# Maxima's rows on ScalarE and GpSimd, a split accumulator copy, additions moved in the tail, and weight slices prepared every five half steps

## The chip, the core and the metric

The kernel runs on one core of a Trainium2 chip. The metric is device time in microseconds of one execution. The core's engines work side by side, each through its own list of instructions in a fixed order: TensorE (PE; its weight loads are shown as PEld), VectorE (DVE), ScalarE (ACT), GpSimd (POOL), and SyncE (SP), which here issues the DMA transfers. An instruction starts when everything ahead of it on its engine has started and the semaphores that it waits for have arrived.

## What is computed

A transformer block with conditioning, for one sequence of 2048 tokens of width 512 in fp32, with 32 heads of 16 and an MLP of width 1792:

```python
mod = (_silu(c) @ w_mod).reshape(c.shape[0], 6, 1, -1)
sa, ca, ga, sb, cb, gb = (mod[:, i] for i in range(6))
h = _layernorm(x) * (1 + ca) + sa
x = x + ga * (softmax((q @ k.T) * 16 ** -0.5) @ v) @ wo      # q, k, v = h @ wqkv, by head
h = _layernorm(x) * (1 + cb) + sb
x = x + gb * (mish(h @ w1 + b1) @ w2)                         # mish(u) = u * tanh(softplus(u))
```

## The kernel before

The products of QKV and MLP are made of fp32 values split in a high and a low part (`hi_copy` and `lo_sub`, lines 93 to 98), three matmuls each.

Attention runs in 512 steps: 32 groups (`n`), one for each of 4 query blocks of 512 and each of 8 groups of 4 heads, with 16 key chunks of 128 each. In step `t` TensorE makes four score products of chunk `t` (L512), four products for the maxima of a later group (L471), which run 20 steps ahead (`PRO`), and the value products of step `t - 2` (L540). Beside the products on half of the array it runs halves of six matmuls of QKV or MLP work (L132). A step is counted in the profile from one bunch of L540 to the next.

The maxima of a group (VectorE, L473) are gathered (`neg_max`), transposed on TensorE (L490) and turned into two rows, high and low part of the negated maximum (`max_rows`: mh L494, mt L495). Four small DMAs (L501) put them into the rows of `qa` that belong to the queries, so that the score product subtracts the maximum by itself: `j` is the pair of heads, `s` the half of the array. The first score of the group uses `j = 0, s = 1`.

When the 16 chunks of a group are added up in a PSUM bank (`acc`), `evac` copies it to `ot` (L554, ScalarE), and DMAs bring sums and rows from `ot` to where the division is made, one or two steps later.

Work that is not TensorE's is hung on half steps, `h = 2t` or `2t + 1` (`at(h, f)`); the order in which hooks run is the order of the instructions on every engine. The weights of the output projection and the MLP are split once, in slices of 128x512 (`prep_unit`): load (L653), three operations on POOL five half steps later (gate L657, L95, L98), and the store to memory (L660) nine half steps after the load. The 32 slices are started by `start_preps`, `PREP = 4` half steps apart, or later where a buffer is not free. The blocks of the MLP (`first_loads`, one for each query block) load them again (L666). `load_pair` brings the keys and queries of a pair of heads (L294, L303).

After the last step `tail` finishes query block 3 alone: attention output, layer norm, MLP. There TensorE also runs ten products that were held back from block 2 (`held`), two at a time into a PSUM pair, each added to `y` by VectorE (L889); `put_h` splits the layer norm's output between them (L712 on ACT, L95 on POOL, L98 on DVE).

Of the kernel before, what the change touches and what calls it, by code (L numbers as in the profile page):

```python
# [18 lines left out]
def adaln_block(ctx: ExitStack, tc: tile.TileContext, x, wqkv, wo, w1, b1, w2, c, w_mod, out):  # L19
    nc = tc.nc  # L20
    P = 128
# [18 lines left out]
    CUT1, CUT2 = (0, 1), (2, 3)  # L40
    LOV = ((1,), (), (1, 3), (1, 3))
    PREP = 4
    CREDIT = 7.5
    HCAP = 10.0

# [439 lines left out]
    def max_rows(n, mm):  # L485
        t = ring(2)
        cols = mm.rearrange("p a v q -> p (a v q)")
        for g in range(2):
            r = slice(64 * g, 64 * g + 64)
            nc.tensor.transpose(t[:32, g, :64], cols[r], ident[r, r])  # L490
        pt = t[:32, :, :64]
        mh, mt = [ap.tile([32, P], F32R, tag=n_, name=n_, bufs=1) for n_ in ("mh", "mt")]
        halves = [m.rearrange("p (g q) -> p g q", g=2) for m in (mh, mt)]
        nc.vector.tensor_scalar_mul(halves[0], pt, -1.0)  # L494
        nc.vector.scalar_tensor_tensor(halves[1], halves[0].bitcast(F32), lows[:32], pt, op0=ALU.mult, op1=ALU.subtract)  # L495

        def put():
            for j in range(2):
                for s in range(2):
                    o = (2 * s + j) * 8  # L500
                    nc.sync.dma_start(  # L501
                        qa[(2 * n + j) % NR][64 * s + 48:64 * s + 50, :].rearrange("v (s q) -> v s q", s=4).bitcast(F32),
                        mt[o:o + 8, :].bitcast(F32))
        at(2 * (16 * n + 16 - PRO) + 3, put)
# [43 lines left out]
    def evac(n):  # L548
        qb, g = divmod(n, G)
        t1 = 16 * (n + 1) + 1  # L550
        if g == 0:
            o_hl[qb] = [ap.tile([P, DK, TB], F32R, tag=f"o_{i}", name="o_hl", bufs=1) for i in range(2)]
        ot = ap.tile([P, TB], F32, tag="ot", name="ot", bufs=1)
        nc.scalar.copy(ot, accs.pop(n))  # L554
# [24 lines left out]
        if g % 2 == 1 or n == NIT - 2:  # L579
            r = slice(0, P if g % 2 else 64)  # L580

            oh, ol = o_hl[qb]
            k, d, e = (2 * t1 + 42, 7, 11) if g == 1 else (2 * t1 + 11, 0, 0) if hurry else (2 * t1 + 23, 4, 8)
            at(k, lambda: nc.gpsimd.tensor_mul(od[r], od[r], rb[r]))
            at(k + d, lambda: hi_copy("p", oh[r, g // 2, :], od[r]))
            at(k + e, lambda: lo_sub("p", ol[r, g // 2, :], od[r], oh[r, g // 2, :]))
# [59 lines left out]
                nc.vector.tensor_copy(modc[:, v - 1, 2 * o:2 * o + 2], acc[:, :2])  # L646
        return fin

    def prep_unit(h, third, scr, src, gate):

        hl = (qp if third else pw).tile([P, 2, D], F32R, tag="vq" if third else "hl", name="hl", bufs=1 if third else 2)
        raw = hl[:, 1, :].bitcast(F32)
        nc.sync.dma_start(raw.rearrange("p (k m) -> p k m", m=src.shape[-1]) if len(src.shape) == 3 else raw, src)  # L653

        def split():
            if gate is not None:
                nc.gpsimd.tensor_mul(raw, raw, gates[gate])  # L657
            hi_copy("p", hl[:, 0, :], raw)
            lo_sub("p", hl[:, 1, :], raw, hl[:, 0, :])
            at(clear(h + 9), lambda: nc.sync.dma_start(scr.rearrange("p v m -> p (v m)"),  # L660
                                                        hl.rearrange("p v m -> p (v m)").bitcast(F32)))
        at(h + 5, split)
# [131 lines left out]
    def block(qb, t0):  # L794
# [8 lines left out]
        def first_loads(h):  # L803
            load(h + 1, wos, load_wo, range(DK))
            load(h + 2, y, lambda i: load_y(qb, i), range(4))
            load(h + 9, w1s, load_w1, range(2))
            load(h + 10, w2s, load_w2, range(NW - DK))
            done["w"] = h + 3

        def wo_unit(i, tag):  # L810
# [179 lines left out]
    def tail():  # L990
# [48 lines left out]
        for k in range(DK):  # L1039
            for i in range(4):  # L1040
                nc.tensor.transpose(accs[k][:, i * P:(i + 1) * P], xn[i][:, k * P:(k + 1) * P], ident)
        for k in range(DK):
            put_h(hh, hl, accs[k], k, True)
        fins += held((6, 7))
        for f in fins:
            f(None)
        for f in held((8, 9)):
            f(None)
        for f in range(6):
            w2s[f] = load_w2(f)  # L1050
        po = [ring(2) for _ in range(2)]
# [3 lines left out]
        for u in range(FT + LAG):  # L1055
# [12 lines left out]
            if f >= 0:  # L1068
                a_h, a_l = act.pop(f)
                w = w2s.pop(f)  # L1070
                for i in range(4):
                    s = slice(i * P, (i + 1) * P)
                    for j, (l, r) in enumerate(((a_h, 0), (a_h, 1), (a_l, 0))):
                        nc.tensor.matmul(po[i // 2][:, i % 2, :], l[:, s], w[:, r, :], start=(f == 0 and j == 0),  # L1074
                                         stop=(f == FT - 1 and j == 2))
                    if f == FT - 1 and i % 2:
                        for q in (i - 1, i):
                            nc.vector.tensor_add(y[q], po[q // 2][:, q % 2, :], y[q])
                            r = 4 * last + q
                            nc.sync.dma_start(out[r * P:(r + 1) * P, :], y[q])  # L1080
                if f + 6 < FT:
                    w2s[f + 6] = load_w2(f + 6)

# [289 lines left out]
```

## Time and profile before

| what | value |
| --- | --- |
| three timed runs | 1693.45, 1697.57, 1698.18 us (median 1697.57) |
| the profiled execution | 1693.26 us, span 1691.5 us |
| granted TensorE clock, mean | 0.996 |
| TensorE busy | 1660.6 us, 98% of the span |
| VectorE, ScalarE, GpSimd busy | 1429.9, 1327.1, 898.0 us |

The span runs from the first to the last instruction; the device time has 1.8 us around it. A row of a timeline gives the start in us, the duration in us, the engine, the line, the operation, what is written and read, the shape and the number of instructions that the row joins; in brackets stands how long the engine was idle ahead of it and what ended that. A row of waits gives the total in us, how many times, and the longest. SPq rows are DMA issues on SP's queue.

### The profile page before, as it was taken

To read this page: it belongs to the slowest core of one execution; us is meant where nothing else is said; L and a number is where in the kernel's file an instruction comes from. 1 tells how busy PE (TensorE), PEld (TensorE's weight loads), DVE (VectorE), ACT (ScalarE), POOL (GpSimd) and SP (SyncE) were. 2 spreads that over 40 slices of the span, in tenths; PEclk is the share of its full clock that TensorE was granted. 3 is DMA by queue.
4 is the path that set the end of the run, shared out by engine and by line. 5 is a ranking of instruction groups with operands and counts; after the bars stand their busy time and mean duration, and the time that the engine had idled before them with its cause. 6 is when DMAs were issued, how large, how long until landed. Compare 5 with 4: busy or idle time off the path is not lost.

```text
span 1691.5 us, 32962 instructions
## 1 busy us (share of the span) xinstructions
PE 1660.6 (98%) x12316; PEld 921.7 (54%) x12316; DVE 1429.9 (85%) x2362; ACT 1327.1 (78%) x2559; POOL 898.0 (53%) x906
## 2 busy tenths in 40 slices
PE   6999999999999999999999999999999999999998
PEld 5755665554435455555555555555555555554687
DVE  6898898887998888988888888889888888881577
ACT  6247777777778898888889898888888898889264
POOL 5155215565504388755525498654535597646432
PEclk9999999999999999999999999999999999999999
DMA  7767457777772342434353644334442535332362
GB/s 249 192 224 215 120 159 213 250 226 226 232 210 63 111 123 74 127 80 149 86 133 74 197 105 99 99 109 123 117 103 79 176 95 131 93 107 82 132 218 74
DMA packets 113992, 240.03 MB, mean 142 GB/s; under 512 B 24048, under 2 KB 49648, under 8 KB 107784
## 3 DMA queue, kind: packets, MB, share of 16 engines
q1 hardware_dynamic: 113832, 237.92, 49.6%
q8 instruction: 97, 1.59, 0.4%
q14 instruction: 63, 0.52, 0.1%
HBM read 179.95 MB, written 51.44 MB: 137 GB/s over the span
## 4 chain that ended last, share of the span: by engine, by line
PE 92%; DVE 3%; DMA 2%; ACT 2%; SPq 1%; issue 1%; POOL 0%; DVEq 0%; ACTq 0%; POOLq 0%
PE bk L540 30%; PE ring L471 23%; PE ring L512 22%; PE bk L132 9%; PE bk L126 3%; PE ring L126 3%; PE ring L1074 2%; DVE mx L473 1%; ACT pr L520 1%; DMA xt<-in_A_x 1%; SPq L318 0%; DMA qa<-mt 0%; PE bk L1006 0%; DMA vg<-vscr 0%; PE ring L842 0%
## 5 line engine op out<-in xcount | busy, mean ns | idle before, releaser
L473 DVE TENSOR_REDUCE mx<-ring 128x1 f32<-128x512 f32 x2048 | 1276.1, 684 | 161.5 <-PE bk L132 104.9
L520 ACT ACTIVATE pr<-ring 128x512 f32<-128x512 f32 x2048 | 1090.2, 605 | 232.0 <-PE bk L132 168.8
L471 PE MATMUL ring<-ka,qa 64*128 64x512 f32 x2048 | 778.7, 427 | 0.5
L512 PE MATMUL ring<-qa,ka 64*128 64x512 f32 x2048 | 723.0, 397 | 7.8 <-ACT pr L520 4.6
L471 PEld LDWEIGHTS ring<-ka,qa 64*128 64x128 f32 x2048 | 366.5, 184 | 407.9 <-DVE mx L473 356.2
L540 PE MATMUL bk<-pr,vg 128*32 128x512 f32 x4096 | 545.9, 605 | 0.0
L512 PEld LDWEIGHTS ring<-qa,ka 64*128 64x128 f32 x2048 | 374.1, 184 | 120.8 <-ACT pr L520 35.6
L132 PE MATMUL bk<-h,w 64*128 64x512 f32 x1008 | 280.7, 410 | 0.0
L132 PE MATMUL bk<-w,a_h 64*128 64x512 f32 x576 | 194.8, 417 | 0.6 <-ACT pr L520 0.4
L132 PEld LDWEIGHTS bk<-h,w 64*128 64x128 f32 x1008 | 171.5, 184 | 5.7 <-ACT pr L520 0.4
L540 PEld LDWEIGHTS bk<-pr,vg 128*32 128x32 f32 x4096 | 81.0, 108 | 125.1 <-issue 117.0
L740 POOL TENSOR_SCALAR ee<-hb 128x512 f32<-128x512 f32 x42 | 62.5, 1488 | 96.7 <-ACT hb L734 88.2
L132 PE MATMUL bk<-w,a_l 64*128 64x512 f32 x288 | 113.7, 395 | 0.0
L770 POOL TENSOR_TENSOR ee<-ee,rr 128x512 f32<-128x512 f32 x42 | 53.9, 1284 | 111.6 <-ACT rr L761 111.4
L132 PEld LDWEIGHTS bk<-w,a_h 64*128 64x128 f32 x576 | 95.3, 185 | 5.2 <-ACT pr L520 1.5
L132 PE MATMUL bk<-w,o_hl 64*128 64x512 f32 x288 | 79.7, 409 | 0.0
L98 POOL TENSOR_TENSOR a_l<-hb,a_h 128x512 fp32r<-128x512 f32 x53 | 71.7, 1354 | 4.4
L893 POOL TENSOR_TENSOR y<-yd,y 128x512 f32<-128x512 f32 x40 | 51.4, 1285 | 35.5 <-ACT yd L892 35.3
L754 POOL TENSOR_SCALAR rr<-ee 128x512 f32<-128x512 f32 x42 | 26.1, 622 | 60.0 <-ACT ee L746 59.9
L132 PE MATMUL bk<-h_h,wl 64*128 64x512 f32 x168 | 57.5, 423 | 0.0
L95 POOL TENSOR_SCALAR a_h<-hb 128x512 fp32r<-128x512 f32 x53 | 36.3, 684 | 39.9 <-DVE hb L768 38.3
L774 POOL TENSOR_TENSOR hb<-hb,rr 128x512 f32<-128x512 f32 x42 | 54.5, 1298 | 3.3
(205 smaller groups left out, 1840.9 us busy)
## 6 DMA issues: line engine op xcount, KB each, us to landing
ka<-kscr SPq DMA_DIRECT2D x124, 384.0 KB
w<-w2scr SPq DMA_DIRECT2D x56, 512.0 KB
w<-w1scr SPq DMA_DIRECT2D x46, 512.0 KB
vg<-vscr SPq DMA_DIRECT2D x32, 552.0 KB
qa<-qscr SPq DMA_DIRECT2D x124, 100.0 KB
kscr<-qh SPq DMA_DIRECT2D x16, 512.0 KB
qscr<-qh SPq DMA_DIRECT2D x32, 256.0 KB
hl<-in_B_w SPq DMA_DIRECT2D x28, 256.0 KB
```

Of the source, the lines that this page charges most:

```text
L98: (nc.gpsimd if eng == "p" else nc.vector).tensor_sub(lo, src, hi.bitcast(F32))
L126: nc.tensor.matmul(acc, l, r, start=start, stop=stop)
L132: i = nc.tensor.matmul(acc, l[64 * g:64 * g + 64], r[64 * g:64 * g + 64], start=start, stop=stop)
L471: nc.tensor.matmul(pm, qt[64 * s:64 * s + 64, qs * P:(qs + 1) * P], kt[64 * s:64 * s + 64, kb * TB:(kb + 1) * TB], start=True, stop=True)
L473: return nc.vector.tensor_reduce(out=mxs[n][:, s, 4 * j + qs, kb:kb + 1], in_=pm, op=ALU.max, axis=AX.X)
L512: nc.tensor.matmul(p_, kt[64 * s:64 * s + 64, kc * P:(kc + 1) * P], qt[64 * s:64 * s + 64, :], start=True, stop=True)
L520: e = nc.scalar.activation(pr, p_, AF.Exp, scale=SCALE)
L540: nc.tensor.matmul(accs[n][32 * h:32 * h + 32, :], vgs[n][:, o:o + 32], pts.pop((t, h)), start=(kc == 0), stop=(kc == 15))
L740: nc.gpsimd.tensor_scalar_min(buf("ee", 2), b["hb"], HCAP)
L770: nc.gpsimd.tensor_mul(ee, ee, rr)
L774: nc.gpsimd.tensor_mul(hb, hb, rr)
L893: nc.gpsimd.tensor_add(y[i], yd, y[i])
```

## The change

It has these parts.

- `max_rows`: the negated rows are copied by ScalarE from PSUM, and mh and mt are then made by POOL (two operations of 32x128) in place of two operations on VectorE. Of the four DMAs those for `s = 1` are issued first.
- `evac`: the first 256 columns of the accumulator are copied by VectorE, the others by ScalarE.
- `tail`: the additions of the held products 4 and 5 stand before `put_h` and those of 6 and 7 behind it, and each output row tile is added when its own products are done.
- `start_preps`: `EARLY = 28` slices, five half steps apart (the first six as before); the last four are prepared when the MLP's memory is open, from half step 256 on, in tiles of their own.
- The keys of group 8's first pair are loaded 8 half steps sooner, and block 0's slices of w1 and w2 20 half steps later.

```diff
     def max_rows(n, mm):
 ...
-        halves = [m.rearrange("p (g q) -> p g q", g=2) for m in (mh, mt)]
-        nc.vector.tensor_scalar_mul(halves[0], pt, -1.0)
-        nc.vector.scalar_tensor_tensor(halves[1], halves[0].bitcast(F32), lows[:32], pt, op0=ALU.mult, op1=ALU.subtract)
+        mc = mt.bitcast(F32)
+        nc.scalar.activation(mc.rearrange("p (g q) -> p g q", g=2), t[:32, :, :64], AF.Copy, scale=-1.0)
+        nc.gpsimd.tensor_scalar_mul(mh, mc, lows[:32])
+        nc.gpsimd.tensor_add(mt, mc, mh.bitcast(F32))

         def put():
-            for j in range(2):
-                for s in range(2):
+            for s in (1, 0):
+                for j in range(2):
...
-        nc.scalar.copy(ot, accs.pop(n))
+        acc = accs.pop(n)
+        nc.vector.tensor_copy(ot[:, :TB // 2], acc[:, :TB // 2])
+        nc.scalar.copy(ot[:, TB // 2:], acc[:, TB // 2:])
...
-    def prep_unit(h, third, scr, src, gate):
+    def prep_unit(h, third, scr, src, gate, hl=None):
-        hl = (qp if third else pw).tile(...)
+        hl = hl if hl is not None else (qp if third else pw).tile(...)
...
         def first_loads(h):
-            load(h + 9, w1s, load_w1, range(2))
-            load(h + 10, w2s, load_w2, range(NW - DK))
+            late = 20 if qb == 0 else 0
+            load(h + 9 + late, w1s, load_w1, range(2))
+            load(h + 10 + late, w2s, load_w2, range(NW - DK))
...
     def tail():
+        for f in fins:
+            f(None)
         for k in range(DK):
             put_h(hh, hl, accs[k], k, True)
-        fins += held((6, 7))
-        for f in fins:
-            f(None)
-        for f in held((8, 9)):
-            f(None)
+        for js in ((6, 7), (8, 9)):
+            for f in held(js):
+                f(None)
...
-                    if f == FT - 1 and i % 2:
-                        for q in (i - 1, i):
-                            nc.vector.tensor_add(y[q], po[q // 2][:, q % 2, :], y[q])
+                    if f == FT - 1:
+                        nc.vector.tensor_add(y[i], po[i // 2][:, i % 2, :], y[i])
...
-        if i == len(preps):
+        if i == EARLY:
-        then = clear(max(h + PREP, puts[0] + 1 if len(puts) > 2 - (not three) else 0))
+        then = clear(max(h + (PREP if not three else 5), puts[0] + 1 if len(puts) > 2 - (not three) else 0))
...
     def prep_step(t):
+            room = [mst["p"].tile([P, 2, 2, D], F32R, tag=f"h2_{v}", name="late", bufs=1) for v in range(2)]
+            for i, args in enumerate(preps[EARLY:]):
+                h = 2 * t + 12 + 3 * i
+                at(h, lambda h=h, i=i, args=args: prep_unit(h, False, *args, room[i // 2][:, i % 2]))
...
-            at(32 * (n - 2) + (15 if n % 2 == 0 else 9), lambda n=n: load_pair(2 * n))
+            at(32 * (n - 2) + (7 if n == 8 else 15 if n % 2 == 0 else 9), lambda n=n: load_pair(2 * n))
```

The order of the instructions shows where these stand. First SP around the maxima's rows of group 6. `hl` is a weight slice (loaded from `in_B_w`, stored to `w2scr`), `qa<-mt` are the rows, `qscr` and `kscr` hold queries and keys. Before:

```order
L660 DMA w2scr<-hl 128x1024
L458 DMA vg<-vscr 128x1104
L252 DMA qscr<-ql 8x16x512
L252 DMA qscr<-qh 8x16x512 x2
L653 DMA hl<-in_B_w 128x512
L660 DMA w2scr<-hl 128x1024
L501 DMA qa_108<-mt 2x4x128 x2
L501 DMA qa_109<-mt 2x4x128 x2
```

After:

```order
L459 DMA vg<-vscr 128x1104
L253 DMA qscr<-ql 8x16x512
L253 DMA qscr<-qh 8x16x512 x2
L663 DMA w2scr<-hl 128x1024
L656 DMA hl<-in_B_w 128x512
L502 DMA qa_108<-mt 2x4x128
L502 DMA qa_109<-mt 2x4x128
L502 DMA qa_108<-mt 2x4x128
L502 DMA qa_109<-mt 2x4x128
```

Between two groups' rows SP issues fewer slices, a load stands directly ahead of the rows where a store stood, and the rows of the two pairs alternate.

POOL in a block, around the same rows of group 11. `hb`, `rr` and `ee` are the pieces of mish, `a_h` and `a_l` the parts of its result. Before:

```order
L773 TENSOR_TENSOR hb<-hb,ee 128x512
L774 TENSOR_TENSOR hb<-hb,rr 128x512
L740 TENSOR_SCALAR ee<-hb 128x512
L95 TENSOR_SCALAR a_h<-hb 128x512
L98 TENSOR_TENSOR a_l<-hb,a_h 128x512
```

After:

```order
L776 TENSOR_TENSOR hb<-hb,ee 128x512
L777 TENSOR_TENSOR hb<-hb,rr 128x512
L495 TENSOR_SCALAR mh<-mt,lows 32x128
L496 TENSOR_TENSOR mt<-mt,mh 32x128
L743 TENSOR_SCALAR ee<-hb 128x512
L96 TENSOR_SCALAR a_h<-hb 128x512
L99 TENSOR_TENSOR a_l<-hb,a_h 128x512
```

The two new operations stand in the middle of the mish of two tiles.

ScalarE at the copy of group 10's accumulator (`bk` is the bank), with the semaphores that each instruction waits for: DMAHW is a DMA queue, the others are engines. Before:

```order
L520 ACTIVATE pr_0_1182<-ring 128x512 [waits PE_49]
L554 COPY ot<-bk 128x512 [waits DMAHW4_49,DMAHW5_49,DMAHW3_49,DMAHW6_49,DMAHW2_49,PE_49]
L520 ACTIVATE pr_2_1151<-ring 128x512 [waits PE_49]
L758 ACTIVATE rr<-ee,two 128x512 [waits Pool_49]
L520 ACTIVATE pr_2_1159<-ring 128x512 [waits PE_49]
```

After:

```order
L521 ACTIVATE pr_0_1183<-ring 128x512 [waits PE_49]
L557 COPY ot<-bk 128x256 [waits DMAHW4_49,DMAHW5_49,DMAHW3_49,DMAHW6_49,DMAHW2_49,DVE_49]
L521 ACTIVATE pr_2_1152<-ring 128x512 [waits PE_49]
L761 ACTIVATE rr<-ee,two 128x512 [waits Pool_49]
L521 ACTIVATE pr_2_1160<-ring 128x512 [waits PE_49]
```

The half copy keeps the place of the whole one. It waits for VectorE (its half, L556) where the whole copy waited for TensorE.

Last, VectorE in the tail: `y` additions of held products and the four subtractions of `put_h`. Before:

```order
L889 TENSOR_TENSOR y_5265<-ring,y_5265 128x512
L889 TENSOR_TENSOR y_5266<-ring,y_5266 128x512
L98 TENSOR_TENSOR h_17735<-hf_17766,h_17734 128x512
L98 TENSOR_TENSOR h_17735<-hf_17770,h_17734 128x512
L98 TENSOR_TENSOR h_17735<-hf_17774,h_17734 128x512
L98 TENSOR_TENSOR h_17735<-hf_17778,h_17734 128x512
L889 TENSOR_TENSOR y_5267<-ring,y_5267 128x512
L889 TENSOR_TENSOR y_5268<-ring,y_5268 128x512
```

After:

```order
L893 TENSOR_TENSOR y_5280<-ring,y_5280 128x512
L893 TENSOR_TENSOR y_5281<-ring,y_5281 128x512
L99 TENSOR_TENSOR h_17797<-hf_17830,h_17796 128x512
L99 TENSOR_TENSOR h_17797<-hf_17834,h_17796 128x512
L99 TENSOR_TENSOR h_17797<-hf_17838,h_17796 128x512
L99 TENSOR_TENSOR h_17797<-hf_17842,h_17796 128x512
L893 TENSOR_TENSOR y_5278<-ring,y_5278 128x512
L893 TENSOR_TENSOR y_5279<-ring,y_5279 128x512
```

The additions to `y_5267` and `y_5268` (after: `y_5280`, `y_5281`) moved from behind the subtractions to ahead of them. TensorE's list of matmuls is the same before and after.

More of the change, by code (lines that the diff above doesn't have):

```diff
@@ L42, in adaln_block @@
     PREP = 4
+    EARLY = 28
     CREDIT = 7.5
@@ L490, in max_rows @@
             nc.tensor.transpose(t[:32, g, :64], cols[r], ident[r, r])
-        pt = t[:32, :, :64]
         mh, mt = [ap.tile([32, P], F32R, tag=n_, name=n_, bufs=1) for n_ in ("mh", "mt")]
-        halves = [m.rearrange("p (g q) -> p g q", g=2) for m in (mh, mt)]
-        nc.vector.tensor_scalar_mul(halves[0], pt, -1.0)
-        nc.vector.scalar_tensor_tensor(halves[1], halves[0].bitcast(F32), lows[:32], pt, op0=ALU.mult, op1=ALU.subtract)
+        mc = mt.bitcast(F32)
+        nc.scalar.activation(mc.rearrange("p (g q) -> p g q", g=2), t[:32, :, :64], AF.Copy, scale=-1.0)
+        nc.gpsimd.tensor_scalar_mul(mh, mc, lows[:32])
+        nc.gpsimd.tensor_add(mt, mc, mh.bitcast(F32))
         def put():
-            for j in range(2):
-                for s in range(2):
+            for s in (1, 0):
+                for j in range(2):
                     o = (2 * s + j) * 8
@@ L647, in mod_unit @@
         return fin
-    def prep_unit(h, third, scr, src, gate):
-        hl = (qp if third else pw).tile([P, 2, D], F32R, tag="vq" if third else "hl", name="hl", bufs=1 if third else 2)
+    def prep_unit(h, third, scr, src, gate, hl=None):
+        hl = hl if hl is not None else (qp if third else pw).tile([P, 2, D], F32R, tag="vq" if third else "hl", name="hl", bufs=1 if third else 2)
         raw = hl[:, 1, :].bitcast(F32)
@@ L1075, in tail @@
                                          stop=(f == FT - 1 and j == 2))
-                    if f == FT - 1 and i % 2:
-                        for q in (i - 1, i):
-                            nc.vector.tensor_add(y[q], po[q // 2][:, q % 2, :], y[q])
-                            r = 4 * last + q
-                            nc.sync.dma_start(out[r * P:(r + 1) * P, :], y[q])
+                    if f == FT - 1:
+                        nc.vector.tensor_add(y[i], po[i // 2][:, i % 2, :], y[i])
+                        r = 4 * last + i
+                        nc.sync.dma_start(out[r * P:(r + 1) * P, :], y[i])
                 if f + 6 < FT:
```

## Prediction

> **What bounds the kernel now.** I read the list of what TensorE waited for first, then the timeline at those places, then the windows, then steps of the attention loop that differ by one instruction only. The page gives the engines' shares, the second view TensorE's waits:
>
> ```profile
> PE 1660.6 (98%) x12316; PEld 921.7 (54%) x12316; DVE 1429.9 (85%) x2362; ACT 1327.1 (78%) x2559; POOL 898.0 (53%) x906
> PE ring L512 <- DMA qa<-mt: 2.5, 1, 2.5
> PE ring L126 <- DVE y L889: 2.4, 1, 2.4
> ```
>
> TensorE is busy 98% of the span and gets the same matmuls in the same order after the change, so only holes in its row can be won or lost. Two are long. The first, at group n=6 (DVE and POOL rows, then SP, then PE):
>
> ```profile
> 377.31 0.34 DVE L495 SCALAR_TENSOR_TENSOR mt<-mh,lows,ring 32x128 fp32r<-32x128 f32 x1 [0.28 <-DVE mh L494]
> 380.57 1.30 POOL L98 TENSOR_TENSOR ql<-ql,qh 128x512 fp32r<-128x512 f32 x1
> 380.71 0.67 SPq L660 DMA_DIRECT2D w2scr<-hl  x1
> 381.51 4.63 SPq L501 DMA_DIRECT2D qa<-mt  x4
> 384.39 0.64 PE L540 MATMUL bk<-pr,vg 128*32 128x512 f32 x4
> 388.43 0.50 PE L512 MATMUL ring<-qa,ka 64*128 64x512 f32 x1 [2.50 <-DMA qa<-mt]
> 390.67 1.93 PE L540 MATMUL bk<-pr,vg 128*32 128x512 f32 x8
> 394.42 1.07 PE L540 MATMUL bk<-pr,vg 128*32 128x512 f32 x8
> ```
>
> The rows of maxima (mt) were ready at 377.65, but SP issued their four DMAs only from 381.51, behind the store of a weight slice, and the score matmul waited 2.50. A step runs from one group of L540 to the next: these two took 6.28 and 3.75, where an ordinary one takes 2.84 (669.11 to 671.95 below). They lose 10.03 − 5.68 = 4.35 us, more than the wait. The second hole is in the tail:
>
> ```profile
> 1599.11 0.69 DVE L98 TENSOR_TENSOR h<-hf,h 128x512 fp32r<-128x512 f32 x1 [3.96 <-POOL h L95]
> 1603.34 2.48 DVE L889 TENSOR_TENSOR y<-ring,y 128x512 f32<-128x512 f32 x4
> 1604.08 0.98 PE L126 MATMUL ring<-w,a_h 128*128 128x512 f32 x2 [2.42 <-DVE y L889]
> 1608.54 2.94 PE L126 MATMUL bk<-h,ka 128*128 128x512 f32 x12
> 388.40:392.40 4.00, 3.97 (x20) 1.55 (x20) 1.98 (x3) 2.17 (x4) 3.83 (x5) 0.61 1.03 193
> 600.90:657.30 56.40, 56.40 (x442) 29.87 (x434) 50.51 (x87) 51.07 (x100) 53.92 (x50) 1.00 0.37 99
> 1604.00:1608.70 4.70, 4.62 (x13) 3.66 (x14) 2.51 (x5) 0.00 (x0) 0.00 (x0) 0.64 0.38 139
> ```
>
> The last three rows are windows; after the busy times of PE, PEld, DVE, ACT and POOL stand the granted TensorE clock, the DMA share and GB/s. Behind both holes the clock is 0.61 and 0.64, against 1.00 in an undisturbed stretch: the slow matmuls there belong to the price of the wait. The Trainium skill (TensorE: Matmul & The Clock Gate, Part 1) puts the fall after an idle window of about 3.4 us. By that, waits of 2.50 and 2.42 would leave the clock alone, and removing them would bring 4.9 us of the 8.35 that the two holes cost. The rows here disagree with it, and I go by them.
>
> **The change part by part.** *SP and the weight slices.* Slices every five half steps, with a buffer reused two half steps later, take the blocked store away from ahead of the maxima's rows; row s=1, which the first score needs, now goes first. This can bring 0 to 4.35. But mt now comes from POOL. In the order of POOL it stands behind the ql row above, which ended at 381.87; with 0.9 for the two new instructions it would be ready at 382.8, with SP free, where the four DMAs began at 381.51 and the second of them released TensorE at 388.4. Only because the prepared slices lie farther apart will POOL be earlier there. I take 3.7: most of it, as the fall of the clock goes with even a partly shortened wait.
>
> *Tail.* The two y additions that free the PSUM pair for the waiting matmuls move ahead of the four subtractions, into the 3.96 us in which VectorE idled until 1599.11. So the 12 matmuls start where TensorE went idle, 1604.08 − 2.42 = 1601.66, and run at full clock: what took 4.46 at 0.64 takes 2.85 (the 12 behind, at 1608.54, take 2.94 with the end of the last). The next 12 start at 1604.51 in place of 1608.54: 4.0 (0 to 4.0). Their h is ready when the subtractions end, before 1604.1. The additions at the very end, one row tile at a time, cover nothing that TensorE waits for: 0.
>
> *Maxima's rows.* An ordinary step, and one with the transposes of the maxima:
>
> ```profile
> 654.72 1.06 PE L540 MATMUL bk<-pr,vg 128*32 128x512 f32 x8
> 655.71 0.23 PE L490 MATMUL ring<-ident,mm 64*32 64x64 f32 x2
> 656.01 0.28 DVE L494 TENSOR_SCALAR mh<-ring 32x128 fp32r<-32x128 f32 x1
> 656.33 0.34 DVE L495 SCALAR_TENSOR_TENSOR mt<-mh,lows,ring 32x128 fp32r<-32x128 f32 x1
> 656.66 1.09 ACT L520 ACTIVATE pr<-ring 128x512 f32<-128x512 f32 x2 [0.33 <-PE ring L512]
> 657.75 0.64 PE L540 MATMUL bk<-pr,vg 128*32 128x512 f32 x4
> 669.11 1.06 PE L540 MATMUL bk<-pr,vg 128*32 128x512 f32 x8
> 671.95 1.06 PE L540 MATMUL bk<-pr,vg 128*32 128x512 f32 x8
> ```
>
> 3.03 against 2.84: 0.19, in which VectorE gave up 0.62. The transposes stay; I leave them half their 0.23, so 0.075 a step and 2.4 over 32 groups is won (0 to 6.1). ScalarE's new copy of 32x128, estimated at 0.25 from 0.374 for 128x256 below, fits its idle 0.33; without that cover it would cost like the copy in the next part, 0.2 a group.
>
> POOL gets two instructions of at most 0.452 each (the row of L850 below is four times as many partitions), 0.9 a group. POOL is 53% busy in all, but 53.92 of 56.40 in the window above, and this returns in three of the four blocks. POOL's first new instruction also waits for ScalarE's copy, with slices, products and mish pieces queued behind it; where POOL comes late, as at n=6, that wait is nothing, elsewhere POOL has idle time to give. In the dense windows 0.9 is handed on to the activations that wait for POOL: 0 to 2.7 in all; I take 1.4, as part of the lag is made up before TensorE needs the products.
>
> *The copy of the accumulator.* One copy on ScalarE becomes two halves, VectorE and then ScalarE. As built, the second half waits for the first. Two evacuations, and the copy prices:
>
> ```profile
> 621.89 2.50 DVE L473 TENSOR_REDUCE mx<-ring 128x1 f32<-128x512 f32 x4 [0.34 <-PE bk L132]
> 623.20 1.06 PE L540 MATMUL bk<-pr,vg 128*32 128x512 f32 x8
> 624.67 0.60 ACT L554 COPY ot<-bk 128x512 f32<-128x512 f32 x1
> 625.14 0.63 ACT L520 ACTIVATE pr<-ring 128x512 f32<-128x512 f32 x1
> 626.25 1.07 PE L540 MATMUL bk<-pr,vg 128*32 128x512 f32 x8
> 667.80 2.50 DVE L473 TENSOR_REDUCE mx<-ring 128x1 f32<-128x512 f32 x4 [0.36 <-PE bk L132]
> 670.24 0.59 ACT L554 COPY ot<-bk 128x512 f32<-128x512 f32 x1 [0.15 <-PE bk L540]
> 670.88 0.60 ACT L520 ACTIVATE pr<-ring 128x512 f32<-128x512 f32 x1
> L272 ACT COPY vq<-bk 128x256 f32<-128x256 f32 x28 | 10.5, 374 | 22.1 <-PE bk L126 22.1
> L892 DVE COPY yd<-bk 128x512 f32<-128x512 f32 x1 | 0.7, 690 | 10.0 <-PE ring L512 10.0
> L850 POOL TENSOR_SCALAR hf<-hf,modc 128x128 f32<-128x128 f32 x48 | 21.0, 452 | 3.9 <-ACT hf L847 3.5 <-PE bk L132 0.2 <-PE ring L471 0.2
> ```
>
> The step at 623.20 lasts 3.05: its first exponential behind the copy starts 1.94 after the step's start, and the last ring slot comes late by 0.21. At 669.11 that exponential starts 1.77 in, and nothing is lost. A VectorE half is 0.42 (0.690 times 0.374/0.605, ScalarE's ratio of the two sizes; 0.605 is L554's mean). At 623.20 VectorE is free at 624.39, its half ends 624.81, ScalarE's at 625.2: the exponential starts where it did, nothing won. At 669.11 VectorE is free at 670.30, the halves end at 670.72 and 671.1, and the exponential moves from 670.88 to 671.14, 2.03 in: now this step loses 0.21 as well. So the change gives at best the present state and at worst 31 × 0.21 = 6.5. Some ten of the steps have no loss or half of it now; I take +2.0. VectorE's own 0.42 is nearly covered by its 0.34 of idle time a step.
>
> The rule behind this: the Trainium skill (PSUM — Partial Sum Buffer, PSUM bank collisions raise a hardware error) states that two engines may not touch one bank and partition quadrant at once, two reads included. It speaks against a split by columns, as here: without it the halves would run together, end at 0.42 in place of 0.60, and this term would be a gain of up to 31 × 0.18 = 5.6.
>
> *The rest at nothing.* The four last slices run on POOL beside block 0's start, where POOL is nearly idle:
>
> ```profile
> 465.00:507.00 42.00, 39.06 (x254) 15.72 (x248) 38.03 (x65) 31.21 (x62) 3.18 (x3) 1.00 0.74 213
> ```
>
> Each is some 3.2 (multiply, round, subtract: 1.3 + 0.6 + 1.3), 13 of 39 idle microseconds; if one stood ahead of a late product of the attention output it could cost 3.2. The later loads of block 0's slices and the earlier key load move on SP's queue while the DMA share is 0.74; a load that came late would cost like n=6, up to 4.35.
>
> Sum: −3.7 − 4.0 − 2.4 + 1.4 + 2.0 = −6.7. The profiled execution took 1693.3, so 1686.6. The three timed runs lie at 1693.45, 1697.57 and 1698.18; the profiled one stands with the fastest, and the sum against their median would be 1690.9. I give 1687, since what makes two runs longer is not in this profile.
>
> **Rivals.** (a) *The stall at n=6 stays*, with POOL holding the rows in SP's place. For it: the ql row and 382.8 above, and DMAs that needed some 6 us from the first issue. Against it: the wider spacing. 1693.3 − 3.0 = 1690.3. (b) *POOL is late for the maxima's rows in blocks.* At n=11 (19 and 27 are alike) mt now stands behind this row of POOL, and the score that needs it is this one:
>
> ```profile
> 613.83 1.30 POOL L774 TENSOR_TENSOR hb<-hb,rr 128x512 f32<-128x512 f32 x1
> 618.86 0.39 PE L512 MATMUL ring<-qa,ka 64*128 64x512 f32 x1
> ```
>
> Ready at 615.13 + 0.9 = 616.03, 2.8 before the score. If a DMA takes longer than that to land, TensorE waits in three groups; with the clock's fall each costs up to 4.35, 13 in all: 1686.6 + 13 = 1699.6, slower than the profiled 1693.3. Against it: the DMA share is 0.37 there, not the load at n=6. (c) *The small terms pay in full*: 4.35 + 4.0 at the holes, 6.1 at the maxima, nothing lost at the copy or on POOL: 1678.9.
>
> **How the numbers follow.** My forecast 0.55; (a) 0.20; (b) 0.07; (c) 0.13; a mixture that ends at no change 0.05. The range goes from 1679 (under c) to 1694 (a, with the timed runs' spread of 4). About 0.3% (5 us) is what can be told from no change, so faster means under 1692.5: nearly all of forecast and (c), and two thirds of (a), 0.78; slower means above 1702.7, where (b) and a late load go: 0.05; the rest is the same.
>
> **What would show it.** Right: the waits on qa<-mt and on y gone from TensorE's list, clock 1.00 in both windows; steps with transposes at about 2.95; ScalarE's half starting only when VectorE's ended, and steps at the copy near 3.05 throughout; POOL over 54 of 56 in the block's dense window. Wrong: a wait on qa<-mt at n=5, 6, 7, 11, 19 or 27; ScalarE's copy beginning beside VectorE's; a new wait on w1scr or w2scr loads.

## The result, and the profile after

The changed kernel takes 1686.12 us (median of 4 runs, 1685.80 to 1688.34), the kernel before 1697.03 in the same comparison (1693.45 to 1698.18). The ratio is 0.9932, with a 95% interval from 0.9915 to 0.9949. The prediction gave 1687 (1679 to 1694). The span of the profiled execution fell from 1691.5 to 1684.2. The median fell by 10.9 and the profiled execution by 7.2 (1693.26 to 1686.03): the one profiled before stands with the fastest of the kernel before, as the prediction says, and the other runs of that kernel are longer.

The list of what TensorE waited for (total, times, longest) has lost both long waits, on qa<-mt and on y. The second of the rows below was 0.4 before, and the three behind it are new:

```profile
PE ring L513 <- ACT pr L521: 5.2, 22, 0.7
PE bk L133 <- ACT pr L521: 1.2, 1, 1.2
PE bk L133 <- ACT yd L896: 1.2, 2, 0.6
PE ring L472 <- DVE mx L474: 0.7, 1, 0.7
PE ring L472 <- ACT pr L521: 0.5, 3, 0.2
```

At n=6 (POOL, SP, PE, and a window over the two steps) the rows of maxima are ready on POOL at 379.11 and SP issues their DMAs at once; the first score begins at 384.96 without a wait, and the clock is 1.00 where it was 0.61:

```profile
376.71 1.29 POOL L99 TENSOR_TENSOR ql<-ql,qh 128x512 fp32r<-128x512 f32 x1
378.66 0.45 POOL L496 TENSOR_TENSOR mt<-mt,mh 32x128 fp32r<-32x128 f32 x1
374.06 1.69 SPq L663 DMA_DIRECT2D w2scr<-hl  x1
379.13 2.77 SPq L502 DMA_DIRECT2D qa<-mt  x4
383.63 1.06 PE L541 MATMUL bk<-pr,vg 128*32 128x512 f32 x8
384.96 0.39 PE L513 MATMUL ring<-qa,ka 64*128 64x512 f32 x1
386.59 0.64 PE L541 MATMUL bk<-pr,vg 128*32 128x512 f32 x4
383.60:389.40 5.80, 5.80 (x46) 2.98 (x44) 5.07 (x10) 5.04 (x12) 5.55 (x6) 1.00 0.88 167
```

In the tail VectorE makes the additions at 1593.57 and 1594.97, before the subtractions, and TensorE runs through:

```profile
1593.57 0.69 DVE L893 TENSOR_TENSOR y<-ring,y 128x512 f32<-128x512 f32 x1 [0.37 <-PE ring L127]
1594.97 0.69 DVE L893 TENSOR_TENSOR y<-ring,y 128x512 f32<-128x512 f32 x1 [0.72 <-PE ring L127]
1602.10 2.89 PE L127 MATMUL bk<-h,ka 128*128 128x512 f32 x12
1596.00:1602.00 6.00, 6.00 (x31) 4.99 (x30) 3.54 (x6) 2.42 (x4) 3.22 (x4) 1.00 0.01 3
```

Since TensorE's matmuls are the same in all kernels here, each one's span can be cut at the starts of the bunches of value products (L540, later L541) and compared step by step. Step `k` runs from bunch `k` to the next one; the tail is counted from the start of bunch 511 to the end of the last matmul. Sums in us, worked out from the PE rows:

| steps | before | after | difference | predicted |
| --- | --- | --- | --- | --- |
| n=6: 93 and 94 | 10.03 | 5.80 | −4.23 | −3.7 |
| tail | 115.73 | 111.05 | −4.68 | −4.0 |
| with transposes, 16n − 6 (31, and step 506, which has none and takes 2.12 in both) | 97.39 | 92.44 | −4.95 | −2.4 |
| with the accumulator's copy, 16n + 15 (31) | 91.38 | 92.37 | +0.99 | +2.0 |
| in the blocks: 173, 301, 429 | 8.51 | 10.32 | +1.81 | +1.4 for all eight |
| 177, 305, 433 | 8.86 | 10.41 | +1.55 | (in the row above) |
| 253 and 381 | 5.68 | 7.96 | +2.28 | (in the row above) |
| 129 and 496 | 6.12 | 6.38 | +0.26 | 0 |

These differences add up to −7.0; all steps and the tail together went from 1576.1 to 1569.6, or by −6.5. What stands ahead of step 0 took 0.4 less; it varies from 109.2 to 113.0 over all profiles here, so each span below is to be read with its start.

Two readings of these rows. A group's rows on ScalarE and POOL (step 202, which fell from 3.03 to 2.92) and two evacuations (steps 175 and 191):

```profile
695.19 1.07 PE L541 MATMUL bk<-pr,vg 128*32 128x512 f32 x8
696.56 0.25 ACT L494 ACTIVATE mt<-ring 32x128 f32<-32x128 f32 x1
696.92 0.60 POOL L495 TENSOR_SCALAR mh<-mt,lows 32x128 fp32r<-32x128 f32 x1
697.60 0.45 POOL L496 TENSOR_TENSOR mt<-mt,mh 32x128 fp32r<-32x128 f32 x1
698.11 0.64 PE L541 MATMUL bk<-pr,vg 128*32 128x512 f32 x4
618.63 0.42 DVE L556 COPY ot<-bk 128x256 f32<-128x256 f32 x1
619.08 0.37 ACT L557 COPY ot<-bk 128x256 f32<-128x256 f32 x1
664.99 0.42 DVE L556 COPY ot<-bk 128x256 f32<-128x256 f32 x1
665.45 0.37 ACT L557 COPY ot<-bk 128x256 f32<-128x256 f32 x1 [0.60 <-DVE ot L556]
```

The second half of the copy starts 0.04 after the first has ended, and in the second case ScalarE stood idle for 0.60 until then. Now each of these steps in the blocks takes 2.94 or 2.95, where they took 2.83 to 3.05. In the blocks the sum even fell, by 0.6; what the copy cost, 1.6, lies in the steps of groups 0 to 7, ahead of the blocks (47, for example, went from 3.22 to 3.47). There ScalarE stood idle for 0.3 to 0.9 in front of its half, at n=11, 19 and 27 for 0.6, and elsewhere for 0.17 at most.

The price in the blocks reads off the chain that ended last (start, length, what) at n=11: POOL's two operations, the mish piece behind them, the activation that needs it, the exponential queued behind that, and the score that needs its ring slot.

```profile
608.86 0.60 POOL mh L495
609.53 0.45 POOL mt L496
610.07 1.50 POOL ee L743
611.59 0.63 ACT ee L749
612.22 0.50 ACT pr L521
612.76 0.49 PE ring L513
```

POOL's share of the dense window did not rise: over the same length of time, from the same step on, it is 53.83 where it was 53.92.

```profile
594.60:651.00 56.40, 56.14 (x432) 29.43 (x426) 49.48 (x82) 50.62 (x100) 53.83 (x52) 1.00 0.39 99
```

Steps 167 to 185, which make up most of it, took 55.2 in place of 54.4. POOL had hardly any idle time left to give, so the new operations made the stretch longer.

At n=16, ahead of step 253, it is another thing: POOL stood idle in front of the two operations, until ScalarE had copied the rows.

```profile
833.66 0.60 POOL L495 TENSOR_SCALAR mh<-mt,lows 32x128 fp32r<-32x128 f32 x1 [8.38 <-ACT mt L494]
834.34 0.45 POOL L496 TENSOR_TENSOR mt<-mt,mh 32x128 fp32r<-32x128 f32 x1
834.75 1.26 POOL L773 TENSOR_TENSOR ee<-ee,rr 128x512 f32<-128x512 f32 x1
831.35 0.62 ACT L764 ACTIVATE rr<-rr 128x512 f32<-128x512 f32 x1
840.67 1.28 POOL L897 TENSOR_TENSOR y<-yd,y 128x512 f32<-128x512 f32 x1
841.98 0.59 ACT L896 COPY yd<-bk 128x512 f32<-128x512 f32 x1 [1.43 <-POOL y L897]
```

The mish piece L773 behind them had its input at 831.97 and began 2.8 us later. Of this, 1.7 is POOL's idle time and 1.1 the two operations. The addition to y at the end of that chain then kept ScalarE's copy waiting 1.43, with exponentials behind it, and TensorE waited 0.58 for the copy (the row of yd in the list above; its other wait is the one at n=24).

### The profile page after: what moved, and what is told of

It is laid out like the page before. It is cut to its first block, busy times and chain, and to the rows that moved or that the text cites. A ratio compares the mean times of both kernels' runs of the same rounds, so it can differ in the third digit from the quotient of the medians.

```text
span 1684.2 us, 33102 instructions
## 1 busy us (share of the span) xinstructions
PE 1655.4 (98%) x12316; PEld 925.5 (55%) x12316; DVE 1427.3 (85%) x2330; ACT 1327.9 (79%) x2591; POOL 928.3 (55%) x970
## 4 chain that ended last, share of the span: by engine, by line
PE 84%; POOL 5%; DVE 3%; ACT 3%; issue 2%; DMA 2%; SPq 0%; POOLq 0%; ACTq 0%; DVEq 0%
PE bk L541 27%; PE ring L472 22%; PE ring L513 20%; PE bk L133 6%; PE bk L127 3%; PE ring L127 3%; ACT pr L521 2%; PE ring L1078 2%; DVE mx L474 1%; DMA ka<-kscr 1%; POOL rr L775 1%; POOL ee L773 1%; POOL hb L776 1%; POOL ee L743 1%; POOL hb L777 1%
## 5 line engine op out<-in xcount | busy, mean ns | idle before, releaser
L541 PE MATMUL bk<-pr,vg 128*32 128x512 f32 x4096 | 545.1, 604 | 0.0
L541 PEld LDWEIGHTS bk<-pr,vg 128*32 128x32 f32 x4096 | 80.9, 108 | 124.7 <-issue 116.7
L773 POOL TENSOR_TENSOR ee<-ee,rr 128x512 f32<-128x512 f32 x42 | 53.8, 1282 | 71.8 <-ACT rr L764 71.6
L495 POOL TENSOR_SCALAR mh<-mt,lows 32x128 fp32r<-32x128 f32 x32 | 19.1, 596 | 81.4 <-ACT mt L494 81.2
L758 POOL TENSOR_TENSOR ee<-ee,rr 128x512 f32<-128x512 f32 x42 | 54.0, 1286 | 3.5
```

Of the source, the lines that this page charges most:

```text
L541: nc.tensor.matmul(accs[n][32 * h:32 * h + 32, :], vgs[n][:, o:o + 32], pts.pop((t, h)), start=(kc == 0), stop=(kc == 15))
L758: nc.gpsimd.tensor_mul(ee, ee, rr)
L773: nc.gpsimd.tensor_mul(ee, ee, rr)
```

## Experiments

The theory was: the gains are the two holes and VectorE's relief; the loss is POOL's, and it takes back most of what the rows give.

**The rows on VectorE again.** The changed kernel with this edit:

```diff
-        nc.scalar.activation(mc.rearrange("p (g q) -> p g q", g=2), t[:32, :, :64], AF.Copy, scale=-1.0)
-        nc.gpsimd.tensor_scalar_mul(mh, mc, lows[:32])
-        nc.gpsimd.tensor_add(mt, mc, mh.bitcast(F32))
+        pt = t[:32, :, :64]
+        halves = [m.rearrange("p (g q) -> p g q", g=2) for m in (mh, mt)]
+        nc.vector.tensor_scalar_mul(halves[0], pt, -1.0)
+        nc.vector.scalar_tensor_tensor(halves[1], halves[0].bitcast(F32), lows[:32], pt, op0=ALU.mult, op1=ALU.subtract)
```

> The changed kernel, with the maxima's rows made on VectorE again (two operations of 0.28 and 0.34 us from PSUM); the rest stays changed. Theory (POOL's time): the steps that grew in the blocks (0.6 at steps 173, 301 and 429, 0.4 to 0.7 at 177, 305 and 433, 1.15 at 253 and 381, 5.6 us in all) return to 2.84, and the steps with the transposes (step 16n - 6) grow again by what they lost, 5.0 us in all, to 3.03; the span stays within 1.5 us of the changed kernel's 1684.2. Rival (the halved copy or the moved slices make those steps longer): they stay long, and the span grows by 5.

Span 1684.6. The eight steps in the blocks sum to 23.04, as before the change (28.69 with it), step 496 is back at 2.78 (3.64), and the steps with transposes are back at 97.0. So moving the rows off VectorE everywhere cost 5.7 + 0.9 and brought 4.6: by these steps it lost 2.0. The two spans differ by 0.4 only, since here step 0 began 1.4 later and step 9 took 1.2 longer, with a wait of 1.15 for keys (step 9 varies between profiles of other kernels here too, from 2.8 to 3.8).

**POOL's time alone.** The kernel before, with work on POOL that nobody waits for:

```diff
...
         mh, mt = [ap.tile([32, P], F32R, tag=n_, name=n_, bufs=1) for n_ in ("mh", "mt")]
         halves = [m.rearrange("p (g q) -> p g q", g=2) for m in (mh, mt)]
+        for c in range(4):
+            nc.gpsimd.tensor_add(spare, ident[:32, 32 * c:32 * c + 32], lows[:32].to_broadcast([32, 32]))
```

> The kernel before, with four additions of 32x32 on POOL (about 1 us together, written to a tile that nobody reads) where the changed kernel makes the maxima's rows; the rows stay on VectorE. It adds work to what the kernel computes. Theory (POOL's time alone is the price): steps 173, 301 and 429, 177, 305 and 433, and 253 and 381 grow as in the changed kernel, 4 to 6 us in all, and the span is about 1691.5 + 5 = 1696.5. Rival (the price is ScalarE's extra copy, or rows that come late): none of these steps grows, span 1691.5 within 1.

Span 1698.9. The four additions took 0.228 each. Steps 173, 301 and 429 grew to 3.34, 3.31 and 3.33, steps 177, 305 and 433 to 3.30, 3.29 and 3.32: 2.5 us, from POOL's time alone, where the changed kernel lost 3.4 with 1.05 a group in place of 0.91. Steps 253 and 381 did not grow (2.84 and 2.83). The theory holds for the first six and fails for these two, and 2.5 is less than the 4 to 6 that I expected. The rest of the longer span lies elsewhere: 2.2 us at n = 5, 6 and 7, 0.7 at step 129, and a start that took 1.9 longer.

**POOL's operations later, at two groups.** The changed kernel, for groups 16 and 24:

```diff
+        def make():
+            nc.gpsimd.tensor_scalar_mul(mh, mc, lows[:32])
+            nc.gpsimd.tensor_add(mt, mc, mh.bitcast(F32))
+        if n in (16, 24):
+            at(2 * (16 * n + 16 - PRO) + 2, make)
+        else:
+            make()
```

> The changed kernel, with POOL's two operations on the rows of groups 16 and 24 two half steps later in POOL's order, behind the mish of the tile that stood behind them; nothing else moves. Theory (there POOL stood idle 8.4 us in front of rows that ScalarE had not copied yet, with ready mish pieces behind them): steps 253 and 381 return from 3.98 to 2.84 to 3.1, about 2 us in all; 173, 301 and 429 stay at 3.45, 496 at 3.64. Rival (the time of the two operations itself makes these steps long): 253 and 381 stay above 3.6.

Steps 253 and 381 are 2.83: at these two it was POOL's waiting in order, not its time (the run before this one gave POOL 0.91 of work there, and these steps did not grow). But the span is 1692.3. Steps 257 to 259 took 15.3 where they took 8.5, and 385 and 386 took 11.0 in place of 5.7. From SP's and VectorE's timelines:

```profile
837.60 2.77 SPq L508 DMA_DIRECT2D qa<-mt  x4
840.42 0.87 SPq L675 DMA_DIRECT2D w<-w2scr  x2
842.96 0.89 SPq L675 DMA_DIRECT2D w<-woscr  x2
846.57 0.61 SPq L574 DMA_DIRECT2D sm<-ot  x1
854.54 0.25 DVE L584 RECIPROCAL rc<-sm 128x16 f32<-128x16 f32 x1 [4.20 <-DMA sm<-ot]
```

SP waited for the later rows until 837.6, so four loads of 512 KB went out behind them, and the 8 KB of sums that VectorE's reciprocal waits for were issued 3.6 us behind the last two of these (in the changed kernel 7.7). They landed only 8 us later, with VectorE's maxima queued behind the reciprocal. At n=24 the same rows show 8 KB issued 3.6 us behind the loads, and again nearly 8 us until they landed. A stall went, and a transfer that it had covered came late; that the bulk loads ahead of it held it up is read from these two places, and no run tested it.

**The weight slices alone.** The kernel before with the changed `start_preps`, `prep_step`, `prep_unit`, `first_loads` and key load, and nothing else (the diffs of these parts above).

> The kernel before with the wider spacing of the weight slices alone (28 of them five half steps apart, the last four in the MLP's memory, block 0's slices loaded later, the key load sooner); rows on VectorE in their old DMA order, whole copy, old tail. Theory (SP's queue held the rows): the wait on qa<-mt at n=6 is gone and steps 93 and 94 are 2.84 and 2.83, span 1691.5 - 4.2 - 0.6 (step 129, whose sums land sooner) = 1686.7. Rival (it is the order of the four DMAs that helps): steps 93 and 94 stay above 8 us together.

Steps 93 and 94: 2.96 and 2.84; step 129: 2.74 (3.35 before). The span is 1687.8, and would be 1686 without a start that took 1.8 longer than in the first profile. The spacing removes the wait at n=6 by itself. The tail, which is that of the kernel before, took 114.10 in place of 115.73, though it has the same wait; the last section says why.

**The order of the four DMAs alone**, in the kernel before:

```diff
-            for j in range(2):
-                for s in range(2):
+            for s in (1, 0):
+                for j in range(2):
```

> The kernel before with the four DMAs of the maxima's rows in the new order alone (s = 1 first). Theory (SP's queue): the row that is needed comes first in place of second, one issue of some 0.7 to 1.2 us sooner, but all four lay behind the same traffic: the wait at n=6 shrinks by at most 1.2 and steps 93 and 94 take 8 to 10 us together (10.03 before). Rival: the order alone removes the wait, 5.7 together.

Steps 93 and 94 took 7.02, less than I expected, and yet the span grew to 1696.7: there were waits at n=5 (step 77: 4.39) and at n=7 (steps 109 and 110: 12.0 in place of 5.7), where the first profile has none. That a better order should make n=7 late by 6 us is no sensible story; so the kernel before was profiled again.

**The kernel before, once more**, and the changed kernel once more.

> The kernel before, unchanged, profiled once more. Theory (SP's queue runs so late in the stretch of the weight slices that small differences in the DMAs' progress decide who waits): the waits on qa<-mt fall differently from the first profile, with steps 77, 93 and 109 (first scores of n = 5, 6, 7) taking 8.5 to 17 us in all (12.0 in the first profile), and this carries most of the spread of the timed runs (1693 to 1698). Rival (the stall at n = 6 is fixed, and the spread lies elsewhere): steps 93 and 94 take 10.0 again, 77 and 109 2.9 and 2.8.

> The changed kernel, unchanged, profiled and timed once more beside the others. Theory (with the wider spacing SP is no longer late): steps 77, 93 and 109 at 2.85 to 3.0 again, and the timed runs within 2 us of each other and of 1686. Rival: a wait on qa<-mt shows in one of the three.

Before: step 77 took 4.09 (2.89 in the first profile), 93 and 94 took 9.36 (10.03), with a wait on qa<-mt at each of the two groups. Steps 77, 93 and 109 took 13.0 together, inside the 8.5 to 17 that I expected. So with slices four half steps apart it is chance who waits at n = 5 to 7. Steps 77, 93, 94, 109 and 110 together took 18.6, 19.1, 23.4, 20.8 and 19.0 in the five profiles with that spacing (the fourth has POOL's extra work), and 14.3 to 14.4 in all eight with the wider one, the changed kernel's second profile among them. That profile has one wait on qa<-mt, of 1.0, but at the very start, at group 0. Sixteen timed or profiled runs of the kernel before lay between 1693.2 and 1700.2, nine of the changed one between 1685.8 and 1688.3; how much of the wider spread is this was not measured run by run. The gain of the order alone can't be read from its one run.

**The old order in the changed kernel** (the edit above, turned round).

> The changed kernel with the four DMAs of the maxima's rows in their old order. Theory (the spacing removed the wait, the order is worth what one issue takes, 0.7 us, and there is more slack than that): steps 93 and 94 stay at 2.96 and 2.84, and the span within 1 us of the changed kernel's. Rival (the rows come just in time on POOL, 2.8 us before the score in the blocks, and the order saves them): waits on qa<-mt at n = 11, 19 and 27, with steps 173, 301 and 429 longer than 3.45 by 0.3 to 0.7 each.

Here the rival was right in the blocks. Steps 173, 301 and 429 took 3.92, 3.93 and 3.93 in place of 3.45, with three waits on qa<-mt from 420 us on:

```profile
PE ring L513 <- DMA qa<-mt: 0.8, 3, 0.3
```

The next steps won it back in part (177, 305 and 433: 8.86 in place of 10.41), so the sum over the six is 20.63 against 20.73: the order decides where TensorE waits, and not how long. Steps 93 and 94 stayed at 2.96 and 2.83.

**The tail alone**, in the kernel before.

> The kernel before with the tail's new order of additions alone. Theory: the tail goes from 115.73 to 111.05 as in the changed kernel (minus 4.7), everything ahead of it stays as before apart from the changing waits at n = 5 to 7; the wait on y is gone. Rival (the tail was helped by what came before it): 112.5 or more.

The wait on y is gone. From the first of the 16 transposes in the tail (L1041) to the first product of the next layer took 7.33 (1600.27 to 1607.60), as in the changed kernel, and 11.58 before. The tail in all was 112.06, between the theory and its rival: the mish and output products behind that point took 1.0 longer than in the changed kernel, and 0.6 longer than before, for a reason that I did not find. These products take 78.3 in every run of the changed kernel and its variants, and 78.3 to 79.3 in the runs that build on the kernel before, at a granted clock of 1.00 in all of them.

**Two mixtures.** The rows on VectorE for the groups at which POOL is dense or waits, and then also the copy by group:

```diff
+        if n in (11, 12, 16, 19, 20, 24, 27, 31):
+            ...                                   (the two operations on VectorE)
+        else:
             nc.scalar.activation(mc.rearrange("p (g q) -> p g q", g=2), t[:32, :, :64], AF.Copy, scale=-1.0)
...
+        if n < 8 or n in (11, 19, 27):
+            nc.scalar.copy(ot, acc)
+        else:
             nc.vector.tensor_copy(ot[:, :TB // 2], acc[:, :TB // 2])
```

> The changed kernel, with the maxima's rows of the groups 11, 12, 16, 19, 20, 24, 27 and 31 on VectorE again, of the others on ScalarE and POOL as changed. Theory (the loss in the blocks is POOL's, by its time at 11, 19 and 27 and by its waiting for ScalarE's copy at 16 and 24): the long steps (173, 177, 253, 301, 305, 381, 429, 433) and step 496 return, minus 5.6 and minus 0.9, the eight steps with transposes give back about 0.3: span 1684.2 - 6.2 = 1678.0. Rival (what one group saves on POOL the next pays): no more than half of that, span 1681 or above.

> As the mixed rows, and also the whole accumulator copied by ScalarE for the groups 0 to 7, 11, 19 and 27, by halves for the others. Theory (the second half waits for the first, so the halved copy ends later than the whole one wherever ScalarE is on time; where ScalarE is late it ends sooner): the evacuation steps of these groups return to what they were, 1.8 us in all: span 1678.0 - 1.8 = 1676.2. Rival (the halved copy's loss comes from VectorE's delay, which moves elsewhere): the span stays at 1678.

The first took 1682.26 (1680.70 to 1683.07), ratio to before 0.9916 (0.9897 to 0.9934); the eight steps are at 23.04, 496 at 2.78, and the steps with transposes at 92.99, so nearly all of their gain stays. The second took 1680.49 (1679.92 to 1680.55), ratio 0.9906 (0.9888 to 0.9923); its copy steps sum to 90.39 (92.3), 1.9 less, as expected. The changed kernel took 1687.67 (1685.93 to 1688.00) beside them, ratio 0.9943 (0.9924 to 0.9963). The second mixture is faster than both kernels. The spans, 1679.9 and 1678.7, are some 2 us above what I expected, since the start took 2 longer there (step 0 began at 112.6 and 112.8; in the first profile of the changed kernel at 110.8).

## Why the prediction was right, point by point

The time came out within 1 us, and the holes were won in the way foretold. The maxima's rows were not: they were to win 1.0 in all (−2.4 + 1.4) and lost 1.6.

**The two holes.** The mechanism was as told, both sizes somewhat larger. At n=6 the wait went wholly and not in part: −4.23 for −3.7. It was the spacing that did it, as the run with the spacing alone shows. In the tail −4.68 for −4.0: the restart gave 4.25, and 0.43 came behind it, where I had looked for nothing. The same products take 78.3 to 79.3 in the runs that build on the kernel before, so the 0.43 can't be put down to the change. And 1.55 of the 4.25 is the slow clock behind the wait, which the run with the spacing alone, with the same wait, did not have.

**The rows, VectorE's side.** Undersized: −4.95 for −2.4. The failed step is "I leave them half their 0.23": most of the steps went from 3.03 to between 2.85 and 2.92, so most of the 0.19 was VectorE's, and the longer ones (3.10 to 3.27) fell to the same length; only at n=12 and 20, with POOL dense, they rose to 3.18.

**The rows, POOL's side.** The other step that failed: 0 to 2.7 with 1.4 taken, measured 5.6 in the eight steps, and 0.87 more at step 496. Two things were wrong in it. The operations take 0.596 and 0.449 and not 0.9 together, which is a trifle; but what they push back is an activation in ScalarE's fixed order, and the exponentials behind it, so "part of the lag is made up" did not happen at n=11, 19 and 27: the six steps there lost 3.4, for 3.1 of POOL's time. And "elsewhere POOL has idle time to give" was false at n=16 and 24: there POOL waited 8.38, the last 1.7 of it with ready work behind, which cost 2.3 us of TensorE's time in the two steps, which the run with POOL's time alone does not show and the run with the operations moved back removes.

**The copy.** Right in kind: the second half waits for the first, and the steps that lost nothing now lose. The size was 0.99 for 2.0, because a step loses 0.11 and not 0.21, and those that lost 0.21 now lose 0.11: with half of the copy ScalarE gets back to its exponentials a little sooner (this reason is argued from the copy's 0.37 in place of 0.60, and no run tested it). The place was wrong too. The forecast was made on rows of the blocks, and there the halves won 0.6; in the steps of groups 0 to 7, with ScalarE on time, they cost 0.08 to 0.32 each, 1.6 in all. The run with the copy chosen by group gave 1.9 back.

**What was left at nothing.** Step 129 won 0.61 in place of 0: in the kernel before VectorE waited there for sums to land, and with the wider spacing and block 0's later loads the step took 2.73 or 2.74 in all eight profiles. Which of the two does it stays open, since the run with the order alone, which moves neither, shows 2.74 as well, and the other runs that build on the kernel before 3.35 to 4.04. Step 496 lost 0.87, by the rows: it is back with the rows on VectorE. And two signs did not come, POOL over 54 in the dense window (53.83) and 3.05 at the copy (2.95).

So the sum, −6.7, met the span's −7.2 by errors that cancel: the rows came out 2.6 worse than forecast (VectorE's side won twice what I gave it, POOL's side cost more than four times), and against that stand the holes with 1.2, the copy with 1.0 and step 129 with 0.6. That is luck, and so is a part of the absolute time. The sum was set on the fastest run of the kernel before; set on the median of 1697.57, as I also weighed, it would have given 1690.9. What the longer runs lost was no term of the sum. The waits at n = 5 to 7, which the spacing removed, are a part of it that the profiles show.

**The rivals.** (a) did not come, nor (c). (b) asked for late rows at n=11, 19 and 27: with the new order no wait on qa<-mt is there, with the old one there is, up to 0.3 each. The slowing at these places is real, but it came through the activations. Its price of 13 us was far off.

## What to carry to other kernels

An engine off the critical path has two prices: its time where it is dense, and its place in the order where it must wait for something new while ready work stands behind it. Look at both wherever work is moved to it, group by group, since the best home for a small operation changes along the program: the same two edits, chosen by group, took 7 us less than made everywhere (1680.5 against 1687.7). A stall taken away moves everything behind it forward, transfers included; look at what is then issued just behind bulk loads. And where a queue runs late, one profile shows only one of the ways in which it can fall.

## What the runs showed of the hardware

The clock did not fall after every wait. After the same wait of 2.42 in the tail it was 0.64 in the kernel before and 1.00 in the run with the spacing alone; after 2.39 at n=7 it was 1.00 in the run with POOL's time alone, after 3.45 at n=7 it was 0.50 in the run with the order alone.

The traces show what differs. In each of the thirteen profiles the granted clock changes only on a grid of 3.413 us: in the first profile of the kernel before it falls to half at 51.33, 389.25 and 1604.39, which lie 99 and 356 times 3.413 apart, and each time for 3.41. So TensorE's idle time is to be counted in windows of this grid. Here are these windows, to 0.1 us, in the kernel before (n=6), around the wait with the spacing alone, around the one with POOL's time alone, and in the run with the tail alone (n=6); TensorE's busy time is the first one behind the length:

```profile
385.80:389.20 3.40, 0.91 (x8) 0.61 (x8) 0.70 (x2) 0.81 (x3) 2.27 (x3) 1.00 0.66 177
389.20:392.60 3.40, 3.40 (x18) 1.01 (x15) 1.98 (x3) 1.94 (x4) 3.32 (x4) 0.51 1.02 170
1601.88 0.73 PE L127 MATMUL ring<-w,a_h 128*128 128x512 f32 x2 [2.42 <-DVE y L891]
1597.80:1601.20 3.40, 1.66 (x8) 0.99 (x6) 2.05 (x4) 1.46 (x2) 1.75 (x3) 1.00 0.00 0
1601.20:1604.60 3.40, 2.72 (x12) 2.23 (x13) 3.07 (x6) 0.00 (x0) 0.00 (x0) 1.00 0.22 80
1604.60:1608.00 3.40, 3.40 (x16) 2.76 (x15) 0.69 (x1) 0.25 (x1) 0.00 (x0) 1.00 0.82 289
439.78 0.50 PE L515 MATMUL ring<-qa,ka 64*128 64x512 f32 x1 [2.39 <-DMA qa<-mt]
434.60:438.00 3.40, 2.79 (x22) 1.23 (x18) 3.05 (x5) 2.56 (x5) 0.92 (x5) 1.00 0.69 237
438.00:441.40 3.40, 1.62 (x15) 1.18 (x15) 0.94 (x3) 1.09 (x3) 3.04 (x3) 1.00 0.56 137
441.40:444.90 3.50, 3.50 (x32) 1.66 (x30) 3.14 (x6) 2.73 (x6) 3.42 (x5) 1.00 0.94 223
386.50:389.90 3.40, 1.87 (x14) 1.05 (x12) 1.43 (x3) 1.78 (x4) 1.89 (x2) 1.00 0.63 192
389.90:393.30 3.40, 3.40 (x16) 1.10 (x16) 1.76 (x3) 1.72 (x4) 3.23 (x4) 0.50 0.97 186
```

Between the first value product and the last matmul of all profiles, eight windows hold 2.0 to 2.5 of idle time, and half the clock was granted in the window behind each of them (2.50 and 2.42 in the first profile of the kernel before, 2.01 in its second, 2.42 with POOL's time alone, 2.42 and 2.06 with POOL's operations later, 2.54 and 2.03 with the order alone). The two waits of 2.4 that left the clock alone were cut by the grid, into about 1.75 and 0.7 and into 0.65 and 1.75. Below 2.0 the idle time alone does not decide: 1.83 (the kernel before once more) and 1.53 (the tail alone) brought the fall, the two pieces of 1.75 did not, and ahead of the first value product two windows with 0.9 did (the second profiles of both kernels). No threshold can be read from this.

The prediction set the rule of the Trainium skill (TensorE: Matmul & The Clock Gate, Part 1) aside on two rows. The same part says that the window of about 3.4 us runs freely, which would let the fall depend on where a wait lies in it. The grid in the traces agrees with that, though the windows that brought the fall here were not idle throughout: matmuls were busy in them for 0.9 to 2.5 us. No run here varied the place of a wait on purpose, so that the place decides is read from the traces and not tested.

A fall of one window at half the clock costs up to some 1.7 us (an estimate, half of 3.41); behind the wait of 3.45 with the order alone and behind the first of the waits with POOL's operations later (2.68, at n=16) it lasted two windows. In the tail the same wait cost 4.25 in the kernel before and 2.70 in the run with the spacing alone (10.03 from the transposes to the next layer's first product, against 7.33 without a wait).
